# A fused convolution and gated MLP on one core: first chunks' work in larger pieces, a PSUM tile for the warm-up matmuls, and the third chunk's cast ahead of the w_out scaling

## The chip, the cores and the metric

The kernel runs on one core of a Trainium2 chip. The metric is device time in microseconds (us), the median of several runs. For one core no second, slower state of the chip was seen in these runs: all of them are of the state "fast", and only such runs are compared.

Names in the profile: PE is TensorE's matmuls, PEld its weight loads, DVE is VectorE, ACT is ScalarE, POOL is GpSimd, SP is SyncE (which here only issues DMAs). L349 is line 349 of the kernel that was profiled; the changed kernel's lines are shifted by two or more.

## The reference

Two stages. First a causal convolution of seven taps along the sequence, each of eight head groups of 24 channels with its own softmax-normalised weights. Then an MLP with a gate.

```
x: (8, 4096, 192)   weight: (8, 7)   w_in: (192, 2048)   w_out: (2048, 192)   beta: (2048,)
w   = softmax(weight, axis=-1)
out[b, s, c] = sum_k w[c // 24, k] * x_pad[b, s + k, c]      # 6 zero rows in front
h   = out.reshape(32768, 192) @ w_in
g   = h * sigmoid(beta * h)
y   = g @ w_out                                              # (32768, 192), float32
```

## The kernel before

The tokens are worked on in chunks of 512 per half of the batch (two halves at once on the 128 partitions). A step `s` has 16 units `u`. In each unit TensorE computes one block of 128 hidden features of step `s` (`hidden`), and a part of the output of the step before (`output`). The gate is `silu(beta * h)` on ScalarE, so w_out must be divided by beta once; GpSimd does that (`prep_w_out`). The convolution of later chunks is made by VectorE, one instruction a tap, from a transposed bf16 copy of x. That copy is made by DMA: GpSimd issues a cast to a DRAM scratch (`cast`), and SyncE a transposing DMA back (`xpose`).

The first chunk would have to wait long for all of this. So it is split in two half steps (`s = 0` and `s = 1`, 256 tokens each) and its convolution is made by TensorE with diagonal weight matrices; the second chunk's transposes are TensorE's too, and its taps VectorE's. The third chunk (`cast(2)`, `xpose(2)`) is the first to come through the DMA. The code that matters, with cuts marked:

```python
    pc = psum_o.tile([128, 2, TOK], FP32, name="po")

    def fill(n):                                     # warm-up matmuls on zeros
        for _ in range(n):
            nc.tensor.matmul(pc[:, 1, :], zeros[:, 0:128], zeros, start=True, stop=True)

    fill(5)
    ...                                              # six small matmuls: tap weights into pc[:, 0]
    fill(2)
    nc.vector.tensor_copy(ident_b, ident)
    nc.vector.tensor_copy(x0b[:, 0:HB], x0[:, 0:HB])
    cw = consts.tile([128, NG, K], FP32)
    nc.vector.tensor_copy(cw.rearrange("p c k -> p (c k)"), pc[:, 0, 0 : NG * K])
    ...
    for c in range(0, NF, 4):
        prep_w_out(c, 4)                             # GpSimd, w_out / beta
    cast(2)                                          # third chunk
    cast(3)
    ...
    def conv_ops(s):                                 # 21 VectorE instructions, one per tap and group
        ...
    def output(s, u):
        ...
            if fc == NF - 1 and b == 1:              # eviction of a finished output tile
                dst = osb[:, q - 1 : q + 1, :].rearrange("p b d -> p (b d)")
                nc.vector.tensor_copy(dst, po[:, 0, 0 : 2 * D])
                nc.vector.tensor_tensor(dst, po[:, 1, 0 : 2 * D], dst, ALU.add)
        ...
    for s in range(N_ST + 1):
        if s + 2 < N_ST:
            queue.extend(conv_ops(s + 2))
        for u in range(NF):
            if s < N_ST:
                hidden(s, u)
            if s > 0:
                output(s - 1, u)
            next(work, None)                         # first chunks' work in small pieces
            if s > 0:
                pops = 2 - u % 2
            else:
                pops = 0 if u < 5 else 1 if u < 14 else 6
            for _ in range(pops):
                if queue:
                    queue.popleft()()                # puts a tap into VectorE's queue
            if u == 0 and s + 4 < N_CH:
                cast(s + 4)
            if u == 1 and s + 2 < N_CH:
                xpose(s + 2)
```

In these traces VectorE takes up its instructions in the order in which the program gives them: the eviction below, whose data is there at about 35 us, runs at 44.96 us, after the taps that the program puts before it. `pops` decides how many taps of a later chunk stand in VectorE's queue in front of the next eviction.

Of the kernel before, what the change touches and what calls it, by code (L numbers as in the profile page):

```python
# [9 lines left out]
FP32 = mybir.dt.float32  # L10
FP32R = mybir.dt.float32r
BF16 = mybir.dt.bfloat16
# [5 lines left out]
def kernel(  # L18
# [17 lines left out]
    nc = tc.nc  # L36

    B, S, D = x.shape
    H, K = weight.shape
# [3 lines left out]
    NG = D // DG  # L43
    TOK = 512
    NF = F // 128
    PAD = K - 1
    HALO = 16
# [21 lines left out]
    psum_h = ctx.enter_context(  # L69
        tc.tile_pool(name="psum_h", bufs=2, space=bass.MemoryType.PSUM)  # L70
    )
    psum_o = ctx.enter_context(
        tc.tile_pool(name="psum_o", bufs=2, space=bass.MemoryType.PSUM)
    )
# [5 lines left out]
    def new_xt(ch):  # L80
        xt = xt_pool.tile([128, NG, HALO + TOK], BF16, name="xt")
        if ch % CHUNKS == 0:
            nc.vector.memset(xt[:, :, 0:HALO], 0.0)
        xts[ch] = xt
        return xt


    def cast(ch):
        p, c = divmod(ch, CHUNKS)
        r0 = HALO if c == 0 else 0  # L90
        t0 = c * TOK - HALO + r0
        t1 = (c + 1) * TOK
        xd = xd_pool.tile([HALO + TOK, NG, 2, DG], BF16, name="xd")
        for h in range(2):
            nc.gpsimd.dma_start(  # L95
                out=xd[r0:, :, h, :],
                in_=x_v[p, t0:t1, h, :].rearrange("t (c d) -> t c d", c=NG),
            )
        xds[ch] = xd
# [9 lines left out]
    NB = TOK // BLK  # L109
    HB = NB // 2  # L110
    x0 = setup.tile([128, NB, 2, D], FP32)
    x0b = setup.tile([128, NB, 2, D], BF16)
# [16 lines left out]
    zeros = setup.tile([128, TOK], BF16)  # L129
# [17 lines left out]
    def copy_w_in(i):  # L147
        cols = slice(i * FW, (i + 1) * FW)
        nc.vector.tensor_copy(w_in_s[DG : 2 * DG, :, cols], w_in_s[0:DG, :, cols])  # L149
# [12 lines left out]
        fill=0.0,  # L162
# [8 lines left out]
        fill=0.0,  # L171
# [25 lines left out]
    nc.vector.reciprocal(rsum, ssum)  # L197
    nc.vector.tensor_scalar_mul(cw8, cw8, rsum)
    pc = psum_o.tile([128, 2, TOK], FP32, name="po")

    def fill(n):
        for _ in range(n):
            nc.tensor.matmul(pc[:, 1, :], zeros[:, 0:128], zeros, start=True, stop=True)  # L203

    fill(5)
    for c in range(NG):
        nc.tensor.matmul(
            pc[:, 0, c * K : (c + 1) * K],
# [2 lines left out]
            start=True,  # L211
            stop=True,
        )
    fill(2)
    ident_b = setup.tile([128, 128], BF16)
    nc.vector.tensor_copy(ident_b, ident)
    nc.vector.tensor_copy(x0b[:, 0:HB], x0[:, 0:HB])
    cw = consts.tile([128, NG, K], FP32)
    nc.vector.tensor_copy(cw.rearrange("p c k -> p (c k)"), pc[:, 0, 0 : NG * K])

# [3 lines left out]
    def diag_v(c):  # L224
        nc.vector.tensor_tensor(
            diag[:, c, :, :],
            ident.unsqueeze(1).to_broadcast((128, K, 128)),
            cw[:, c, :].unsqueeze(2).to_broadcast((128, K, 128)),
            ALU.mult,
        )  # L230

    def transposes(pt, xb, b0, at, nb):
        for b in range(nb):
            for c in range(NG):
                for h in range(2):
                    nc.tensor.transpose(  # L236
                        pt[h * DG : (h + 1) * DG, c, (at + b) * BLK : (at + b + 1) * BLK],
                        xb[:, b0 + b, h, c * DG : (c + 1) * DG],
                        ident_b,
                    )  # L240

    xt0 = setup.tile([128, NG, HALO + TOK], FP32R)
    nc.vector.memset(xt0[:, :, 0:HALO].bitcast(FP32), 0.0)
    cts = {}

    def diag_tap(s, c, k, pv):
        n = steps[s][2]
        o = HALO - PAD + steps[s][1] + k
        nc.tensor.matmul(  # L249
            pv,  # L250
            diag[:, c, k, :],
            xt0[:, c, o : o + n],
            start=(k == 0),
            stop=(k == K - 1),
        )

    def diag_conv(s, c, pv, ct):
        for k in range(K):
            diag_tap(s, c, k, pv)
        if c == 0:  # L260
            nc.scalar.copy(ct[:, c, 0 : steps[s][2]], pv)  # L261
        else:
            nc.vector.tensor_copy(ct[:, c, 0 : steps[s][2]], pv)

    n0 = HB * BLK
    pt = psum_o.tile([128, NG, n0], BF16, name="po")
    transposes(pt, x0b, 0, 0, HB)
    fill(3)
    diag_v(1)
    nc.scalar.copy(xt0[:, 0:2, HALO : HALO + n0], pt[:, 0:2, :])  # L270
    nc.vector.tensor_copy(xt0[:, 2, HALO : HALO + n0], pt[:, 2, :])
    for k in range(K):
        nc.scalar.mul(diag[:, 0, k, :], ident, cw[:, 0, k : k + 1])
    diag_v(2)
    copy_w_in(0)
    ct = ct_pool.tile([128, NG, TOK], BF16, name="ct")
    cts[0] = ct
    diag_conv(0, 1, psum_h.tile([128, 2, TOK], FP32, name="ph")[:, 0, 0:n0], ct)
    fill(2)
    diag_conv(0, 2, psum_h.tile([128, 2, TOK], FP32, name="ph")[:, 0, 0:n0], ct)  # L280
    beta_p = pc[:, 0, 32 : 32 + NF]
    nc.tensor.transpose(beta_p, beta_q, ident[0:NF, 0:NF])
    beta = consts.tile([128, NF], FP32)
    nc.vector.tensor_copy(beta, beta_p)
    diag_conv(0, 0, psum_o.tile([128, 2, TOK], FP32, name="po")[:, 0, 0:n0], ct)
    beta_r = setup.tile([128, NF], FP32)
    nc.vector.reciprocal(beta_r, beta)
    nc.vector.tensor_copy(x0b[:, HB:NB], x0[:, HB:NB])

    def first_xt():  # L290

        pt = psum_o.tile([128, NG, n0], BF16, name="po")
        transposes(pt, x0b, HB, 0, HB)
        nc.vector.tensor_copy(xt0[:, :, HALO + n0 :], pt)

    def first_conv():

        cts[1] = ct_pool.tile([128, NG, TOK], BF16, name="ct")
        pv = psum_o.tile([128, 4, n0], FP32, name="po")
        for c in range(NG):  # L300
            for k in range(K):
                diag_tap(1, c, k, pv[:, c, :])
                if k % 3 == 2 or k == K - 1:
                    if k == K - 1 and c == NG - 1:
                        nc.vector.tensor_copy(cts[1][:, :, 0:n0], pv[:, 0:NG, :])  # L305
                    yield

    def second_xt():
        xt = new_xt(1)
        pt = psum_o.tile([128, NG, TOK], BF16, name="po")  # L310
        for b in range(NB):
            transposes(pt, x1b, b, b, 1)
            if b == NB - 1:
                nc.vector.tensor_copy(
                    xt[:, :, HALO - PAD : HALO], xt0[:, :, HALO + TOK - PAD :]
                )
                nc.vector.tensor_copy(xt[:, :, HALO:], pt)
            yield
# [3 lines left out]
    def prep_w_out(c0, n):  # L322
        nc.gpsimd.tensor_tensor(  # L323
            w_out_s[:, c0 : c0 + n, :],
            w_out_raw[:, c0 : c0 + n, :],
            beta_r[:, c0 : c0 + n].unsqueeze(2).to_broadcast((128, n, D)),
            ALU.mult,
        )

    for c in range(0, NF, 4):  # L330
        prep_w_out(c, 4)
    cast(2)
    cast(3)


    def conv_ops(s):
        ch, t0, n = steps[s]

        def tap(j, k):
            if j == k == 0:  # L340
                cts[s] = ct_pool.tile([128, NG, TOK], BF16, name="ct")
            o = HALO - PAD + k + t0
            src = xts[ch][:, j, o : o + n]
            dst = cts[s][:, j, 0:n]
            scalar = cw[:, j, k : k + 1]
            if k == 0:
                nc.vector.tensor_scalar_mul(dst, src, scalar)  # L347
            else:
                nc.vector.scalar_tensor_tensor(  # L349
                    out=dst, in0=src, scalar=scalar, in1=dst, op0=ALU.mult, op1=ALU.add  # L350
                )

        return [lambda j=j, k=k: tap(j, k) for k in range(K) for j in range(NG)]
# [59 lines left out]
                )  # L413


    def first_work():

        first_xt()
        copy_w_in(1)
        yield  # L420
        for _ in second_xt():
            yield
        copy_w_in(2)
        for i, _ in enumerate(first_conv()):
            if i == 2:
                copy_w_in(3)
            yield

    work = first_work()
    queue = deque()  # L430
    for s in range(N_ST + 1):
        if s + 2 < N_ST:
# [3 lines that stand above are left out]
                hidden(s, u)  # L436
            if s > 0:
                output(s - 1, u)
            next(work, None)
            if s > 0:  # L440
                pops = 2 - u % 2
            else:
                pops = 0 if u < 5 else 1 if u < 14 else 6
            for _ in range(pops):
                if queue:
                    queue.popleft()()
# [4 lines that stand above are left out]
# [30 lines left out]
```

## Time and profile before

| | before |
|---|---|
| median of the 3 runs | 709.6 us (708.7 to 709.84) |
| profiled span | 708.0 us |
| TensorE busy | 694.0 us (98%) |
| VectorE / ScalarE busy | 78% / 82% |
| first large matmul (step 0) | 13.45 us |
| second half step (step 1) begins | 27.97 us |
| step 2 resumes | 46.16 us |

A kernel whose TensorE is busy 98% can only be gained on where TensorE is idle or slow. The list of waits of TensorE says where; the columns are who waited for whom, us in total, times, and the longest.

```profile
engine line waited for: us in total, times, longest us
PE po L397 <- DVE osb L407: 5.2, 1, 5.2
PE ph L366 <- DVE ct L305: 1.5, 1, 1.5
...
```

The 5.2 us are one wait. The chain of waits (start, us, what) tells what made it. It follows the work back from the end of the program, here from 7.87 to 46.16 us:

```profile
7.87 8.49 DMA w_out_raw<-in_moe_w_out_dram
...
16.50 5.97 POOL w_out_s L323 x4
22.48 1.14 POOL xd L95
23.61 5.14 DMA xd<-in_x_dram
...
28.84 9.91 DMA xt<-xd
...
38.87 0.88 DVE ct L347 x3
39.74 5.30 DVE ct L349 x8
45.04 0.48 DVE osb L406
...
45.55 0.57 DVE osb L407
...
46.16 0.82 PE po L397 x8
```

Read it upwards from the last line. TensorE's output matmuls wait for the eviction L406/L407, which frees their PSUM buffer. The eviction's data had been ready since about 35 us, but in VectorE's queue eleven taps of the third chunk stand in front of it. These wait for the chunk's transpose, that for its cast, and the cast stands in GpSimd's queue behind the scaling of w_out.

VectorE's timeline of the same time (start, us, engine, line, operation, out<-in, count, idle before and releaser) shows both sides of it:

```profile
...
17.34 0.96 DVE L317 COPY xt<-po 128x1536 bf16<-128x1536 bf16 x1 [1.01 <-PE po L236]
18.33 1.61 DVE L149 COPY w_in_s<-w_in_s 64x1536 bf16<-64x1536 bf16 x1
19.97 2.65 DVE L347 TENSOR_SCALAR ct<-xt,cw 128x512 bf16<-128x512 bf16 x2
22.66 0.69 DVE L149 COPY w_in_s<-w_in_s 64x1536 bf16<-64x1536 bf16 x1
...
27.82 8.70 DVE L349 SCALAR_TENSOR_TENSOR ct<-xt,cw,ct 128x512 bf16<-128x512 bf16 x13
38.87 0.88 DVE L347 TENSOR_SCALAR ct<-xt,cw 128x512 bf16<-128x512 bf16 x3 [2.35 <-ACT g L373]
```

It is busy without a gap from 17.34 to 36.5, idle for 2.35 us, and then starts the third chunk's taps. The releaser named there, ScalarE, had been done long before; the DMA transpose landed at 38.74 (in the chain it starts at 28.84 and takes 9.91 us, both rounded), and that is what VectorE waited for. The same copy of w_in takes 1.61 us at 18.33 and 0.69 us at 22.66: in between GpSimd's scaling ended (16.50 to 22.47).

The gap has a second price. TensorE's timeline after it:

```profile
40.16 0.81 PE L366 MATMUL ph<-ct,w_in_s 64*128 64x512 bf16 x6
46.16 0.82 PE L397 MATMUL po<-w_out_s,g 64*128 64x192 bf16 x8 [5.18 <-DVE osb L407]
46.75 1.51 PE L366 MATMUL ph<-ct,w_in_s 64*128 64x512 bf16 x6
...
52.28 0.82 PE L366 MATMUL ph<-ct,w_in_s 64*128 64x512 bf16 x6
```

The same six matmuls take 1.51 us at 46.75 and 0.82 us at 52.28. The granted clock in the windows table is 0.50 from 46.16 to 52.0. The Trainium skill, "TensorE: Matmul & The Clock Gate", section "What's actually happening", says that the array runs at half clock after an idle window of about 3.4 us and at the full one after a busy window; these records agree. Running 5.8 us at half speed costs about 2.9 us, an estimate: half of it.

### The profile page before, as it was taken

How to read it: one execution, taken by the hardware profiler on the slowest of the kernel's cores; microseconds unless marked ns; L12 is line 12 of the kernel's file. 1: busy time of each engine (PE TensorE's matmuls, PEld its weight loads, DVE VectorE, ACT ScalarE, POOL GpSimd, SP SyncE). 2: the span in 40 equal slices, each digit the busy share in tenths (PEclk: the TensorE clock that was granted, in tenths of full speed). 3: DMA queues.
4: the chain of work that ended last, by engine and by line, in shares of the span. 5: the costliest groups of instructions: out<-in, count | busy, mean ns of one | idle time of the engine just before them, and what ended most of it. 6: DMA issues, size and time to landing. Idle time of an engine off the chain costs nothing.

```text
span 708.0 us, 24854 instructions
## 1 busy us (share of the span) xinstructions
PE 694.0 (98%) x11469; PEld 528.7 (75%) x11469; DVE 551.9 (78%) x935; ACT 579.1 (82%) x543; POOL 70.0 (10%) x83
## 2 busy tenths in 40 slices
PE   8979999999999999999999999999999999999997
PEld 5657777777777777777777777777777777777776
DVE  4989988777888777798877788877779887777213
ACT  5759888888888888888888888888888888888881
POOL 6945444000000000000000000000000000000000
PEclk9989999999999999999999999999999999999999
DMA  9999999922213222312222221232221322111012
GB/s 183 107 155 166 172 170 175 134 47 70 60 34 71 69 47 70 68 38 57 69 70 48 69 58 36 69 69 48 69 70 37 57 69 70 47 47 47 24 47 69
DMA packets 181450, 54.57 MB, mean 77 GB/s; under 512 B 146385, under 2 KB 181025, under 8 KB 181345
## 3 DMA queue, kind: packets, MB, share of 16 engines
q0 software_dynamic: 98048, 14.89, 29.4%
q1 hardware_dynamic: 83248, 38.09, 23.1%
q8 instruction: 89, 1.46, 0.9%
q14 instruction: 17, 0.13, 0.1%
q10 hardware_dynamic: 48, 0.01, 0.0%
HBM read 28.98 MB, written 37.29 MB: 94 GB/s over the span
## 4 chain that ended last, share of the span: by engine, by line
PE 93%; DMA 3%; POOL 2%; DVE 1%; issue 0%; POOLq 0%; DVEq 0%; SPq 0%
PE po L397 47%; PE ph L366 46%; DMA xt<-xd 1%; DMA w_out_raw<-in_moe_w_out_dram 1%; POOL w_out_s L323 1%; DVE ct L349 1%; DMA xd<-in_x_dram 1%; POOL w_in_s L142 0%; POOL x1b L117 0%; POOL xd L95 0%; DVE osb L407 0%; DVE osb L406 0%; DVE ct L347 0%; POOL sel L158 0%; POOL sel L167 0%
## 5 line engine op out<-in xcount | busy, mean ns | idle before, releaser
L373 ACT ACTIVATE g<-ph,beta 128x1024 bf16<-128x1024 f32 (+1 forms) x528 | 572.8, 1088 | 106.5 <-PE ph L366 102.2
L397 PEld LDWEIGHTS <-g 64*128 64x128 bf16 x8192 | 370.4, 94 | 108.9 <-issue 7.0
L397 PE MATMUL po<-w_out_s,g 64*128 64x192 bf16 x8192 | 431.5, 243 | 5.2 <-DVE osb L407 5.2
L366 PE MATMUL ph<-ct,w_in_s 64*128 64x512 bf16 (+1 forms) x3168 | 428.9, 372 | 2.0 <-DVE ct L305 1.5
L349 DVE SCALAR_TENSOR_TENSOR ct<-xt,cw,ct 128x512 bf16<-128x512 bf16 x558 | 379.0, 744 | 0.0
L366 PEld LDWEIGHTS <-w_in_s 64*128 64x128 bf16 x3168 | 162.2, 94 | 56.4 <-DVE ct L305 1.8
L406 DVE COPY osb<-po 128x384 f32<-128x384 f32 x128 | 71.4, 558 | 136.3 <-PE po L397 130.5
L407 DVE TENSOR_TENSOR osb<-po,osb 128x384 f32<-128x384 f32 x128 | 71.3, 557 | 4.4
L95 POOL DMA_DIRECT2D xd<-in_x_dram x60 | 54.5, 911 | 45.5 <-DMA xd<-in_x_dram 44.2
L347 DVE TENSOR_SCALAR ct<-xt,cw 128x512 bf16<-128x512 bf16 x93 | 30.2, 379 | 2.4 <-ACT g L373 2.3
L203 PE MATMUL po<-zeros 128*128 128x512 bf16 x12 | 5.9, 629 | 1.3 <-DVE warm L132 1.3
L323 POOL TENSOR_TENSOR w_out_s<-w_out_raw,beta_r 128x768 bf16<-128x768 f32 x4 | 6.0, 1520 | 5.6 <-DMA w_out_raw<-in_moe_w_out_dram 5.6
L249 PE MATMUL po<-xt_145,diag 128*128 128x256 f32 x28 | 6.0, 318 | 0.0
L249 PEld LDWEIGHTS po<-xt_145,diag 128*128 128x128 f32 x28 | 3.9, 188 | 1.9 <-issue 1.9
L149 DVE COPY w_in_s<-w_in_s 64x1536 bf16<-64x1536 bf16 x4 | 3.8, 940 | 0.1
L249 PEld LDWEIGHTS ph<-xt_145,diag 128*128 128x128 f32 x14 | 3.1, 292 | 0.7 <-ACT xt_145 L270 0.3
L249 PE MATMUL ph<-xt_145,diag 128*128 128x256 f32 x14 | 3.6, 419 | 0.0
L203 PEld LDWEIGHTS <-zeros 128*128 128x128 bf16 x12 | 1.2, 130 | 2.6 <-issue 1.3
L261 ACT CAST ct<-po 128x256 bf16<-128x256 f32 x1 | 0.4, 372 | 3.3 <-PE po L249 3.3
L184 POOL DMA_DIRECT2D w_out_raw<-in_moe_w_out_dram x4 | 3.1, 775 | 0.0
L142 POOL DMA_DIRECT2D w_in_s<-in_moe_w_in_dram x4 | 2.6, 673 | 0.8 <-POOLq L465 0.8
L270 ACT CAST xt_145<-po 128x512 fp32r<-128x512 bf16 x1 | 0.6, 585 | 2.3 <-PE po L236 2.3
(45 smaller groups left out, 27.1 us busy)
## 6 DMA issues: line engine op xcount, KB each, us to landing
out_dram<-osb SPq DMA_DIRECT2D x62, 384.0 KB, 3.1
xd<-in_x_dram POOLq DMA_DIRECT2D x54, 198.0 KB, 14.0
w_out_raw<-in_moe_w_out_dram POOLq DMA_DIRECT2D x4, 384.0 KB, 9.1
xd<-in_x_dram POOLq DMA_DIRECT2D x6, 192.0 KB, 15.0
x_83<-in_x_dram SPq DMA_DIRECT2D x4, 192.0 KB, 4.1
w_in_s<-in_moe_w_in_dram POOLq DMA_DIRECT2D x4, 192.0 KB, 7.4
out_dram<-osb SPq DMA_DIRECT2D x4, 192.0 KB, 6.1
xt<-xd SPq DMA_TRANSPOSE x30, 4.9
```

The costliest lines, as they stand in the source:

```text
L95: nc.gpsimd.dma_start(out=xd[r0:, :, h, :], in_=x_v[p, t0:t1, h, :].rearrange("t (c d) -> t c d", c=NG),)
L149: nc.vector.tensor_copy(w_in_s[DG : 2 * DG, :, cols], w_in_s[0:DG, :, cols])
L203: nc.tensor.matmul(pc[:, 1, :], zeros[:, 0:128], zeros, start=True, stop=True)
L249: nc.tensor.matmul(pv, diag[:, c, k, :], xt0[:, c, o : o + n], start=(k == 0), stop=(k == K - 1),)
L323: nc.gpsimd.tensor_tensor(w_out_s[:, c0 : c0 + n, :], w_out_raw[:, c0 : c0 + n, :], beta_r[:, c0 : c0 + n].unsqueeze(2).to_broadcast((128, ...
L347: nc.vector.tensor_scalar_mul(dst, src, scalar)
L349: nc.vector.scalar_tensor_tensor(out=dst, in0=src, scalar=scalar, in1=dst, op0=ALU.mult, op1=ALU.add)
L366: nc.tensor.matmul(ph[:, h, 0:n], w_in_s[rows, j, cols], cts[s][rows, j, 0:n], start=(j == 0), stop=(j == NG - 1),)
L373: nc.scalar.activation(gs[s][:, fc, :, 0:n], ph[:, :, 0:n], AF.Silu, scale=beta[:, fc : fc + 1])
L397: nc.tensor.matmul(po[:, r, b * D : (b + 1) * D], g[rows, fc, h, q * BLK : (q + 1) * BLK], w_out_s[rows, fc, :], start=(fc == 0), stop=(fc ...
L406: nc.vector.tensor_copy(dst, po[:, 0, 0 : 2 * D])
L407: nc.vector.tensor_tensor(dst, po[:, 1, 0 : 2 * D], dst, ALU.add)
```

## The change

Its intent: the first steps are full of small pieces of work between the large matmuls, and each change between them costs TensorE. So the pieces are made larger and fewer. The warm-up matmuls get a PSUM tile of their own, so that the copy of the tap weights need not wait for them. The second half of the first chunk is cast by ScalarE and transposed before the first large matmul. The third chunk's cast is issued ahead of the w_out scaling. The diff, cut to its core:

```diff
     pc = psum_o.tile([128, 2, TOK], FP32, name="po")
+    pf = psum_h.tile([128, 2, TOK], FP32, name="ph")
...
-            nc.tensor.matmul(pc[:, 1, :], zeros[:, 0:128], zeros, start=True, stop=True)
-    fill(5)
+            nc.tensor.matmul(pf[:, 0, :], zeros[:, 0:128], zeros, start=True, stop=True)
+    fill(6)
...
-    fill(2)
     nc.vector.tensor_copy(x0b[:, 0:HB], x0[:, 0:HB])
+    nc.scalar.copy(x0b[:, HB:NB], x0[:, HB:NB])
...
     transposes(pt, x0b, 0, 0, HB)
-    fill(3)
+    fill(2)
...                                   # second half: cast and transposes out of step 0, to here
-    nc.vector.tensor_copy(x0b[:, HB:NB], x0[:, HB:NB])
+    ptb = psum_o.tile([128, NG, n0], BF16, name="po")
+    transposes(ptb, x0b, HB, 0, HB)
+    copy_w_in(0)
-    fill(2)
     diag_conv(0, 2, ...)
     diag_conv(0, 0, ...)
+    nc.vector.tensor_copy(xt0[:, :, HALO + n0 :], ptb)
+    copy_w_in(1)
...
+    cast(2)
     for c in range(0, NF, 4):
         prep_w_out(c, 4)
-    cast(2)
     cast(3)
...                                   # pieces: 12 transposes or 7 taps instead of 6 or 3
+    first_work = {
+        1: more(xt1_work),
+        3: more(xt1_work),
+        4: lambda: copy_w_in(2),
+        5: more(conv1_work),
+        8: lambda: (more(conv1_work)(), copy_w_in(3)),
+        11: more(conv1_work),
+    }
...
-            next(work, None)
+            if s == 0 and u in first_work:
+                first_work[u]()
...
-                pops = 0 if u < 5 else 1 if u < 14 else 6
+                pops = 0 if u < 4 else 1 if u < 12 else 4
```

More of the change, by code (lines that the diff above doesn't have):

```diff
@@ L274 @@
     diag_v(2)
-    copy_w_in(0)
     ct = ct_pool.tile([128, NG, TOK], BF16, name="ct")
@@ L278 @@
     diag_conv(0, 1, psum_h.tile([128, 2, TOK], FP32, name="ph")[:, 0, 0:n0], ct)
-    fill(2)
-    diag_conv(0, 2, psum_h.tile([128, 2, TOK], FP32, name="ph")[:, 0, 0:n0], ct)
     beta_p = pc[:, 0, 32 : 32 + NF]
@@ L284 @@
     nc.vector.tensor_copy(beta, beta_p)
-    diag_conv(0, 0, psum_o.tile([128, 2, TOK], FP32, name="po")[:, 0, 0:n0], ct)
     beta_r = setup.tile([128, NF], FP32)
     nc.vector.reciprocal(beta_r, beta)
-    nc.vector.tensor_copy(x0b[:, HB:NB], x0[:, HB:NB])
-    def first_xt():
-        pt = psum_o.tile([128, NG, n0], BF16, name="po")
-        transposes(pt, x0b, HB, 0, HB)
-        nc.vector.tensor_copy(xt0[:, :, HALO + n0 :], pt)
+    ptb = psum_o.tile([128, NG, n0], BF16, name="po")
+    transposes(ptb, x0b, HB, 0, HB)
+    copy_w_in(0)
+    diag_conv(0, 2, psum_h.tile([128, 2, TOK], FP32, name="ph")[:, 0, 0:n0], ct)
+    diag_conv(0, 0, psum_o.tile([128, 2, TOK], FP32, name="po")[:, 0, 0:n0], ct)
+    nc.vector.tensor_copy(xt0[:, :, HALO + n0 :], ptb)
+    copy_w_in(1)
     def first_conv():
@@ L302, in first_conv @@
                 diag_tap(1, c, k, pv[:, c, :])
-                if k % 3 == 2 or k == K - 1:
-                    if k == K - 1 and c == NG - 1:
-                        nc.vector.tensor_copy(cts[1][:, :, 0:n0], pv[:, 0:NG, :])
-                    yield
+            if c == NG - 1:
+                nc.vector.tensor_copy(cts[1][:, :, 0:n0], pv[:, 0:NG, :])
+            yield
     def second_xt():
@@ L312, in second_xt @@
             transposes(pt, x1b, b, b, 1)
+            if b % 2 == 0:
+                continue
             if b == NB - 1:
@@ L413, in output, with more @@
                 )
-    def first_work():
-        first_xt()
-        copy_w_in(1)
-        yield
-        for _ in second_xt():
-            yield
-        copy_w_in(2)
-        for i, _ in enumerate(first_conv()):
-            if i == 2:
-                copy_w_in(3)
-            yield
-    work = first_work()
+    xt1_work = second_xt()
+    conv1_work = first_conv()
+    def more(work):
+        return lambda: next(work, None)
+    first_work = {
[6 more added lines that the diff above has]
+    }
     queue = deque()
```

## The prediction

> **What bounds the kernel.** TensorE: busy 694.0 of 708.0 us (busy table) and full from 54 us on (stage windows). Only the start can move. The list of waits gives TensorE two long ones after the first large matmul: 1.5 us before 28.0 us (on the second half's convolution) and 5.2 us before 46.16 us. Each is followed by slow matmuls: the eight output matmuls take 0.64 us instead of 0.33, until 31.6 and until 52.1 us (timeline). This fits the Trainium skill, "TensorE: Matmul & The Clock Gate", "What's actually happening": half clock after an idle window, windows of 3.4 us; 31.6 to 52.1 is six of them.
>
> The 5.2 us decide the total. The chain of waits: w_out load lands 16.4, GpSimd scaling 16.5-22.5, cast of the third chunk lands 28.75, its DMA transpose takes 9.9 us to 38.74, then VectorE does 11 convolution taps (38.87-44.96) and the PSUM evictions (to 46.11) queued behind them. VectorE idled 36.5-38.87 for that transpose (the waits view names ScalarE, which was long done). VectorE is busy from 17.34 to 36.5, so other early work hides behind it.
>
> **What the change does.**
> - Cast first: it can be issued at 10.9 instead of 22.4 and should land near 23; even at 9.9 us the transpose ends near 33, before VectorE wants it. The 2.35 us VectorE idle goes.
> - Separate warm-up tile: the weight copy no longer waits for two fills (6.30 -> about 5.4), mostly not realised, because of the next point.
> - x0's second half cast on ScalarE: that load's packets run until nearly 8 us (DMA view), and in ScalarE's order the cast stands before the copy of the first transposes (now 7.09-7.67). I estimate 7.9 + 0.8 (between the 0.58 and 1.09 us that ScalarE takes for 512 and 1024 columns) = 8.7, copy done 9.3: the first diagonal convolution starts near 9.4 instead of 7.88, TensorE idle some 2 us before it. The second half's transposes (0.5-0.85 us, plus about 0.5 waiting for the beta copy to free their PSUM buffer) move ahead of the first large matmul, two fills (0.5) leave. First large matmul: 15-16 us instead of 13.45.
> - Larger pieces: a seven-tap convolution costs 1.0-1.1 us in one piece against 0.55+0.55+0.32 in three; about 1.5 us less TensorE between 13.5 and 26.5. But ScalarE's 16 activations at 0.69 us are 11 us there, so the stage stays near 13 us. VectorE's long stretch starts near 18.5 instead of 17.34.
> - Part of that is absorbed: while GpSimd scales (to 22.5), a VectorE copy took 1.61 us instead of 0.69 and taps 1.1-1.5 instead of 0.35 (Trainium skill, "SBUF — State Buffer", "SBUF: two separate sides": an exclusive port pair). A later start runs fewer of them then.
>
> **Sum.** VectorE ends the second chunk's taps near 37.0 (36.5), goes on at once, evicts near 44.4; TensorE resumes near 44.5 instead of 46.16: -1.7 us. Slow-clock phase after it: shorter or equal, -0.3 on average, +-1. Later nothing changes: 709.6 - 2.0 = 707.6 us, range 705.3 to 709.7. Faster by over 2% 0.01, within 2% 0.98, slower 0.01.
>
> **What would show it.** The transpose issued near 23, landed before 35; no VectorE idle between the second and third chunk's taps; TensorE still idle 4-5 us before about 44.5, ended by the eviction, then slow matmuls; first large matmul later than 13.45 with ScalarE's new cast ending near 8.7.
>
> **What would make it wrong.** The x0 load landing earlier (then the start is 13.0 and the gain nearer 2.5-3 us); the cast's packets delaying the w_out load; the clock staying full over the gap (up to 3 us more gain); w_in's fourth copy coming late and stalling TensorE.

## The result, and the profile after

| | before | after |
|---|---|---|
| median | 709.6 us (708.7 to 709.84, 4 runs) | 707.63 us (707.5 to 708.06, 4 runs) |
| profiled span | 708.0 us | 705.8 us |
| first large matmul | 13.45 us | 15.80 us |
| VectorE's long stretch begins | 17.34 us | 18.66 us |
| third chunk's first tap | 38.87 us | 36.83 us |
| TensorE resumes in step 2 | 46.16 us | 44.12 us |

The ratio is 0.9976 with a 95% interval of 0.9958 to 0.9993. Here and below a ratio is the mean time of one kernel's fast runs over that of the other's of the same rounds, so it is not quite the ratio of the medians that are quoted. The interval does not contain 1, so there is a small gain.

The list of waits and the chain of the kernel after, over the same stretch as above:

```profile
PE po L395 <- DVE osb L405: 4.3, 1, 4.3
PE ph L250 <- ACT xt_146 L271: 2.1, 1, 2.1
PE ph L364 <- ACT g L371: 1.6, 4, 0.5
```

```profile
2.32 5.43 DMA x_83<-in_x_dram
...
8.57 0.59 ACT xt_146 L271
9.20 1.86 PE ph L250 x7
...
15.80 0.52 PE ph L364 x6
...
18.66 0.96 DVE xt L315
...
36.92 0.79 DVE ct L345 x3
...
44.12 0.82 PE po L395 x8
```

The DMAs and the scaling have gone from the end of the chain. In their place stands VectorE's own work, and in front of it the start of the program: TensorE now waits 2.1 us for ScalarE before its first diagonal convolution (L250). ScalarE's timeline shows why:

```profile
7.83 0.83 ACT L218 CAST x0b<-x_83 128x768 bf16<-128x768 f32 x1 [3.08 <-DMA x_83<-in_x_dram]
8.57 0.58 ACT L271 CAST xt_146<-po 128x512 fp32r<-128x512 bf16 x1
```

The new cast L218 waits for the load of x0's second half, and the copy L271 that TensorE needs stands behind it; before, that copy ran at 7.09.

One more thing differs at the start of the two profiles, and no edit aims at it: TensorE's clock. The second and third diagonal convolution of seven matmuls take 1.86 and 1.70 us here (at 11.99 and 13.65), and 1.56 and 1.09 us before (at 10.25 and 11.90). The first clock record in the trace file, at full speed, begins at 15.42 us here and at 11.07 us before; the windows view counts the time ahead of it as full speed.

VectorE's timeline after:

```profile
18.66 0.96 DVE L315 COPY xt<-po 128x1536 bf16<-128x1536 bf16 x1 [2.57 <-PE po L237]
19.65 0.69 DVE L149 COPY w_in_s<-w_in_s 64x1536 bf16<-64x1536 bf16 x1
20.38 2.91 DVE L345 TENSOR_SCALAR ct<-xt,cw 128x512 bf16<-128x512 bf16 x3
...
27.56 9.36 DVE L347 SCALAR_TENSOR_TENSOR ct<-xt,cw,ct 128x512 bf16<-128x512 bf16 x14
36.83 0.88 DVE L345 TENSOR_SCALAR ct<-xt,cw 128x512 bf16<-128x512 bf16 x3
```

There is no idle time before 36.83 any more. The long stretch begins 1.32 us later than before, but ends only 0.4 us later, and the third chunk is tapped 2.04 us earlier, which is just the 2.04 us by which TensorE resumes earlier. After the gap TensorE runs at half clock until 49.55 us (granted clock 0.50 from 44.12 to 49.55), for 5.4 us instead of the 5.9 us of before.

### The profile page after: what moved, and what is told of

The parts are those of the page before. It is cut to its first block, busy times and chain, and to the rows that moved or that the text cites. A ratio compares the mean times of both kernels' runs of the same rounds, so it can differ in the third digit from the quotient of the medians.

```text
span 705.8 us, 24846 instructions
## 1 busy us (share of the span) xinstructions
PE 690.7 (98%) x11465; PEld 530.5 (75%) x11465; DVE 550.1 (78%) x934; ACT 579.2 (82%) x544; POOL 70.3 (10%) x83
## 4 chain that ended last, share of the span: by engine, by line
PE 94%; DVE 4%; DMA 1%; ACT 0%; issue 0%; SPq 0%; ACTq 0%
PE po L395 47%; PE ph L364 46%; DVE ct L347 2%; DMA x_83<-in_x_dram 1%; DVE ct L345 1%; PE ph L250 1%; PE po L250 0%; DVE w_in_s L149 0%; SPq L117 0%; ACT g L371 0%; PE po L237 0%; DVE osb L405 0%; DVE osb L404 0%; DVE xt L315 0%; DVE ct L301 0%
## 5 line engine op out<-in xcount | busy, mean ns | idle before, releaser
L364 PEld LDWEIGHTS <-w_in_s 64*128 64x128 bf16 x3168 | 164.1, 94 | 55.7 <-issue 3.6
L345 DVE TENSOR_SCALAR ct<-xt,cw 128x512 bf16<-128x512 bf16 x93 | 29.9, 377 | 0.0
L250 PE MATMUL ph<-xt_146,diag 128*128 128x256 f32 x14 | 3.7, 439 | 2.1 <-ACT xt_146 L271 2.1
L250 PEld LDWEIGHTS ph<-xt_146,diag 128*128 128x128 f32 x14 | 3.1, 324 | 3.2 <-ACT xt_146 L271 3.0
L204 PE MATMUL ph<-zeros 128*128 128x512 bf16 x8 | 3.8, 627 | 1.3 <-DVE warm L132 1.3
L250 PE MATMUL po<-xt_146,diag 128*128 128x256 f32 x28 | 5.0, 326 | 0.0
L250 PEld LDWEIGHTS po<-xt_146,diag 128*128 128x128 f32 x28 | 4.3, 224 | 0.6 <-issue 0.6
L218 ACT CAST x0b<-x_83 128x768 bf16<-128x768 f32 x1 | 0.8, 831 | 3.1 <-DMA x_83<-in_x_dram 3.1
```

What stands on the lines that cost most here:

```text
L204: nc.tensor.matmul(pf[:, 0, :], zeros[:, 0:128], zeros, start=True, stop=True)
L250: nc.tensor.matmul(pv, diag[:, c, k, :], xt0[:, c, o : o + n], start=(k == 0), stop=(k == K - 1),)
L345: nc.vector.tensor_scalar_mul(dst, src, scalar)
L364: nc.tensor.matmul(ph[:, h, 0:n], w_in_s[rows, j, cols], cts[s][rows, j, 0:n], start=(j == 0), stop=(j == NG - 1),)
```

## The experiments

The theory: the gain is the 2.35 us for which VectorE waited for the third chunk (theory A), and everything else in the first 40 us hides behind VectorE, whose order of work decides when TensorE may go on. The rival: the gain comes from the faster start and the larger pieces (B). Each experiment was timed in five rounds against the kernel before on the same chip. Those that came in one call are in one group; times of different groups are compared by their ratios to before.

### The parts of the change, one at a time

**cast_only** is the kernel before with one edit:

```diff
+    cast(2)
     for c in range(0, NF, 4):
         prep_w_out(c, 4)
-    cast(2)
     cast(3)
```

> Before plus only the third chunk's cast ahead of the w_out scaling. Theory A (the gain is the 2.35 us that VectorE sat idle for the transposed third chunk): no VectorE idle at 36.5 us, eviction near 43.7, TensorE resumes near 43.8 instead of 46.16, total about 707.2 us (706.4 to 708.0), so the whole of the gain or a little more. Rival B (the gain is the faster start and the larger pieces): about 709.6, within 0.5.

Measured: 706.61 us (706.17 to 707.65), ratio 0.9959 [0.9947, 0.9971]. VectorE reaches the third chunk at 36.83 without a gap, TensorE resumes at 44.09. The one moved line gives all of the gain, and B falls as its cause. (A wait of VectorE would stand in brackets at the end of this line.)

```profile
36.83 0.86 DVE L347 TENSOR_SCALAR ct<-xt,cw 128x512 bf16<-128x512 bf16 x3
```

**cast_late** is the other way round: the changed kernel with the cast put back behind the scaling.

> The changed kernel with the cast put back behind the scaling. Theory A: the transposed chunk lands near 39, VectorE idles about 2 us before its first tap on it, TensorE resumes near 46.3, total about 709.6 us (708.9 to 710.3). Rival B: the gain stays, about 707.6.

Measured: 711.25 us (709.38 to 713.45), ratio 1.0023 [1.0007, 1.0038]: slower than before. The gain goes with the cast, as A says, but the loss is larger than was expected:

```profile
42.19 0.88 DVE L345 TENSOR_SCALAR ct<-xt,cw 128x512 bf16<-128x512 bf16 x3 [4.60 <-DMA xt<-xd]
```

VectorE waits 4.6 us, and this time the profile names the DMA. The scaling began later in this run (17.58 instead of 16.91 us after, when the w_out load landed), the transpose was issued at 30.44 and took 11.6 us to land, against 9.9 in the kernel before and 6.9 in the kernel after. In these profiles the transposes that were issued later took longer; that later casts already queued are the reason is plausible and was not tested. The estimate of 39 us for its landing had taken the 9.9 us over.

**own_fill_tile** is the kernel before with the PSUM tile `pf` alone.

> Before with only the warm-up matmuls in a PSUM tile of their own. The weight copy runs at about 6.3 us only if it waits for the fills because of the tile; here it runs near 5.4. TensorE's own queue still runs the fills between, so the first large matmul stays near 13.45 (13.0 to 13.5) and the total at 709.6 us within 0.5, because the transposed chunk lands no earlier. Rival B: 0.9 us less.

Measured: 709.65 us (708.84 to 710.61), ratio 0.9993 [0.9979, 1.0007]. The copy of the weights runs at 5.35 instead of 6.30 us, as intended, and the first large matmul is at 13.59: VectorE then waits 1.06 us for ScalarE instead. A real wait was removed, and nothing was behind it.

**x0_later** is the changed kernel with ScalarE's cast moved behind the copy that TensorE waits for:

```diff
-    nc.scalar.copy(x0b[:, HB:NB], x0[:, HB:NB])
...
     nc.scalar.copy(xt0[:, 0:2, HALO : HALO + n0], pt[:, 0:2, :])
+    nc.scalar.copy(x0b[:, HB:NB], x0[:, HB:NB])
```

> The changed kernel with ScalarE's cast of x0's second half moved behind its copy of the first transposes. First diagonal convolution near 7.0 us instead of 9.20, first large matmul near 13.4 instead of 15.80. Theory A with the port pair: VectorE's long stretch starts 2 us earlier but three or four more of its operations then meet GpSimd's scaling (16.9 to 22.9), so the taps end only 0.3 to 0.6 us earlier and the total is about 707.2 us. Rival C (the later start costs its full 2 us): about 705.4.

Measured: 706.4 us (705.16 to 706.66), ratio 0.9949 [0.9937, 0.996]. The first large matmul is at 11.70 us, 4.1 us earlier than in the changed kernel, and VectorE's long stretch begins at 15.27 instead of 18.66, 3.4 us earlier. But the third chunk's taps begin only 1.0 us earlier, at 35.82, and TensorE resumes at 43.09. More came through than the 0.3 to 0.6 us of the expectation, much less than the full start. Not all of the 4.1 us is the moved cast. The first diagonal convolution of the changed kernel, and then of this one:

```profile
9.20 1.86 PE L250 MATMUL ph<-xt_146,diag 128*128 128x256 f32 x7 [2.08 <-ACT xt_146 L271]
```

```profile
6.37 1.08 PE L249 MATMUL ph<-xt,diag 128*128 128x256 f32 x7 [0.24 <-DVE diag L225]
```

It begins 2.8 us earlier, and the three convolutions take 1.08, 1.11 and 1.04 us instead of 1.86, 1.86 and 1.70: 2.2 us less, because TensorE is at full clock from 4.13 us on (first clock record). Against this stands a wait of 1.19 us at 8.80 for the moved cast. Up to 4.13 us TensorE has the same instructions at the same times in both kernels, so the edit can hardly have brought the early full clock; that it helped to keep it is possible and not shown (evict_first, below, has ScalarE's cast in the old place, reached full clock at 4.74 us and lost it at 8.15, in a wait of 3.17 us for ScalarE). In which of the unprofiled runs the clock was full so early is not known.

Where the other 2.4 us of VectorE's earlier start went can be read off its timeline:

```profile
16.97 2.11 DVE L345 TENSOR_SCALAR ct<-xt,cw 128x512 bf16<-128x512 bf16 x3
19.00 1.95 DVE L347 SCALAR_TENSOR_TENSOR ct<-xt,cw,ct 128x512 bf16<-128x512 bf16 x1
20.98 1.84 DVE L149 COPY w_in_s<-w_in_s 64x1536 bf16<-64x1536 bf16 x1
```

Alone, the three take 0.88, 0.74 and 0.69 us. Here, during GpSimd's scaling (17.46 to 23.88), they take 2.11, 1.95 and 1.84, and one more tap at 22.86 takes 1.58: 4.4 us more than alone. In the changed kernel only the three L345 taps are slowed, by 2.0 us. The difference is the missing 2.4 us.

**no_scaling** takes the suspected cause away: GpSimd's scaling is left out of the changed kernel and w_out is cast to bf16 on its way in. Its output is wrong, which doesn't matter for the time.

> The changed kernel without GpSimd's scaling (w_out is cast on its way in; the result is wrong on purpose). Port pair theory: the three first taps take 0.9 us together instead of 2.91, the eviction comes 2 us earlier, TensorE resumes near 42.1, total about 705.5 us. Rival (those taps are slow for another reason): taps 2.9 us and about 707.6.

Measured: 705.17 us (704.76 to 705.97), ratio 0.993 [0.9917, 0.9943].

```profile
18.71 0.69 DVE L149 COPY w_in_s<-w_in_s 64x1536 bf16<-64x1536 bf16 x1
19.43 1.25 DVE L333 TENSOR_SCALAR ct<-xt,cw 128x512 bf16<-128x512 bf16 x3
```

The three taps take 1.25 us instead of 2.91, and TensorE resumes at 42.49. So most of their slowness was the scaling. The total does not measure it alone: in this profile TensorE's gap before 42.49 was 2.50 us, and the six matmuls after it took 0.83 us, so the half-speed phase is missing too. The rest, 1.25 against 0.88, is not explained by it; GpSimd issues DMAs at that time in this kernel.

### The order of VectorE's work

If taps that stand in front of the eviction are what makes TensorE wait, then moving them behind it should remove the gap itself, where the change only shortened it. **evict_first** is the changed kernel with:

```diff
-            if s > 0:
+            if s == 1:
+                pops = 0 if u < 7 else 1
+            elif s == 2:
+                pops = 1
+            elif s > 0:
                 pops = 2 - u % 2
```

> The changed kernel, but the third chunk's taps are not put into VectorE's queue before the first output eviction of the second stage, and fewer of them before the next two. Theory A: the eviction runs right after the second chunk's taps (36.8), TensorE goes on at 39 without the gap of 4.3 us, its clock stays full (another 2.5 us), total about 700.3 us (699 to 702). Rival D (VectorE's total work early is the bound, not its order): the stall moves to a later stage, total 706 to 708.

Measured: 700.44 us (700.21 to 701.12), ratio 0.9872 [0.9857, 0.9886]. VectorE evicts right after the second chunk's taps, and TensorE goes through without a gap and at full speed:

```profile
37.03 0.55 DVE L404 COPY osb<-po 128x384 f32<-128x384 f32 x1
37.61 0.56 DVE L405 TENSOR_TENSOR osb<-po,osb 128x384 f32<-128x384 f32 x1
38.09 0.87 DVE L345 TENSOR_SCALAR ct<-xt,cw 128x512 bf16<-128x512 bf16 x3
```

```profile
38.92 0.83 PE L364 MATMUL ph<-ct,w_in_s 64*128 64x512 bf16 x6
39.57 0.51 PE L395 MATMUL po<-w_out_s,g 64*128 64x192 bf16 x8
39.90 0.83 PE L364 MATMUL ph<-ct,w_in_s 64*128 64x512 bf16 x6
```

No wait for an eviction is left in TensorE's list. The rival of this experiment (VectorE has too much work, whatever its order) falls: the taps were moved, none was removed.

**before_evict_first** is the kernel before with the same edit, the cast left behind the scaling.

> The kernel before with only the queue order of evict_first. Theory A: without the eviction behind them the taps may wait for the transposed chunk at no cost: TensorE goes on near 40.9 without a long gap, total about 702 us (700.5 to 703), so the cast's place no longer matters. Rival: the chunk still lands at 38.7 and the next stage waits for its taps, total above 706.

Measured: 701.85 us (701.76 to 701.96), ratio 0.9882 [0.9868, 0.9897]. The eviction ends at 37.6. VectorE still waits for the third chunk (2.75 us, until 40.38), but nothing that TensorE needs stands behind that wait, and TensorE's list has no long wait in step 2:

```profile
37.07 0.56 DVE L407 TENSOR_TENSOR osb<-po,osb 128x384 f32<-128x384 f32 x1
40.38 1.24 DVE L347 TENSOR_SCALAR ct<-xt,cw 128x512 bf16<-128x512 bf16 x3 [2.75 <-DMA xt<-xd]
```

So the wait for the transpose was costly only through the queue.

**cast_evict_first** adds the cast's move to that. It is thus evict_first_x0_later, below, without the larger pieces, the fill tile and ScalarE's cast.

> Before plus the cast ahead of the scaling plus the queue order of evict_first; so evict_first_x0_later without the larger pieces, the fill tile and x0's cast on ScalarE. If VectorE's order hid what these parts gain, they show now: TensorE reaches the first half-filled stage's end near 40 us instead of 36.6, total 701 to 702 us against 698.3. If they are worth nothing in themselves: about 698.5.

Measured: 700.67 us (699.94 to 703.96), ratio 0.9858 [0.9841, 0.9874], with a wide scatter; in the profiled run, the slowest, TensorE was at half speed from 28.95 until about 35 us. It is nearer to the first branch of the expectation (701 to 702) than to the second (698.5). It overlaps with before_evict_first (0.9868 to 0.9897), so whether the cast's place is worth anything once the order is right stays open.

**evict_first_x0_later** puts both edits on the changed kernel.

> evict_first and x0_later together. If evict_first takes away the VectorE bound, TensorE's start shows: the second stage begins when VectorE has copied its convolution, 0.3 to 1 us earlier, total 0.5 to 2 us below evict_first, about 699 us. If the port pair eats the earlier start here too, the same as evict_first within 0.5.

Measured: 698.28 us (697.81 to 699.11), ratio 0.9834 [0.9819, 0.985]. That is 2.2 us below evict_first and 2.4 us below cast_evict_first by the medians, 2.7 and 1.7 us by the ratios (0.0038 and 0.0024 of 710). Together, the larger pieces, the fill tile and the earlier start are worth about this much once VectorE's order no longer hides them: step 0 now starts at 11.76 instead of 13.48 and step 2 begins at 36.63. Which of these parts is worth it stays open, since neither the larger pieces nor the moved cast was run alone; and TensorE's clock was full from 4.25 us in this profile and from 11.09 in that of cast_evict_first, a share that is not separated.

**copy_before_taps** adds one more change of order, of three taps that stood in front of the copy of the second half's convolution:

```diff
-                pops = 0 if u < 4 else 1 if u < 12 else 4
+                pops = 0 if u < 4 or 8 <= u < 12 else 1 if u < 8 else 5
```

> evict_first_x0_later, with no taps put into VectorE's queue between the first and the last piece of the second half's convolution, so that its copy runs about 2.9 us earlier. The second stage starts near 24.4 instead of 26.06, where ScalarE's activations end. But VectorE's work up to the eviction (35.2 to 36.3) is the same, so TensorE waits for the eviction instead: total about 698 us, within 0.7 of evict_first_x0_later. If the copy's place were the bound: 696.7.

Measured: 697.18 us (696.43 to 699.4), ratio 0.9818 [0.9798, 0.9838], the fastest of all by its median, though its interval overlaps with that of evict_first_x0_later. The expectation was wrong in one step: it held VectorE's work up to the eviction to be the same. The eviction ended 0.9 us earlier. Evict_first_x0_later first, then copy_before_taps, at the same time of the scaling (which ends at 23.3 and 23.2 us):

```profile
22.24 1.58 DVE L347 SCALAR_TENSOR_TENSOR ct<-xt,cw,ct 128x512 bf16<-128x512 bf16 x1
```

```profile
22.16 0.96 DVE L301 CAST ct<-po 128x768 bf16<-128x768 f32 x1
23.04 0.74 DVE L347 SCALAR_TENSOR_TENSOR ct<-xt,cw,ct 128x512 bf16<-128x512 bf16 x1
```

The copy comes out of PSUM and takes its usual 0.95 us beside the scaling; the tap, run after it, takes 0.74 instead of 1.58.

### The whole change against its best part

**after_again** and **cast_only_again** repeat the changed kernel and cast_only in the same rounds.

> The changed kernel once more, in the same rounds as cast_only_again, to separate the two: 707.6 us (707.2 to 708.2) again. In the profiles of both VectorE reaches the third chunk's first tap at 36.83 us and TensorE resumes at 44.1; what differs is the half-speed phase after it, which ends near 49.1 here and near 47.3 there.

> 706.6 us again (706.1 to 707.7), so about 1 us less than the changed kernel: the parts other than the cast then cost a little as they stand. If the two come out within 0.4 us of each other, the difference was of the chip or the batch.

Measured: 707.28 us (706.54 to 708.36), ratio 0.9971 [0.9955, 0.9986], against 706.38 us (706.08 to 707.43), ratio 0.9957 [0.9942, 0.9972]. The means differ by 0.8 us, in the same direction as in the first group, but the intervals overlap: the other parts as they stand gain nothing, and perhaps cost a little. In both profiles TensorE resumes within 0.1 us of the same time (44.09 and 44.20). What differs is the clock after the gap. In cast_only_again TensorE reached the gap later (41.3 against 39.1 us, after a half-speed phase from 28.9 to 32.4), was idle only 2.9 us and came back at full speed; in after_again it was idle 5.0 us and the next 3.6 us were almost all slow. That a later arrival can be the faster one for this reason is seen in these two profiles, not shown for the medians. The mean clock that each run of after_again lists points to the slow phases too, but not cleanly: two runs at 0.996 took 706.54 and 706.66 us and three at 0.994 took 707.74 to 708.36, yet one at 0.989 took 706.83. (The ends of the slow phases in the expectation, 49.1 and 47.3, are 49.55 and 47.18 in the clock records.)

## Why the prediction was right

The time was predicted as 707.6 us and measured as 707.63. That the two agree to 0.03 us is luck: the four runs spread over 0.56 us, and the median of the kernel before moves between 709.59 and 710.7 us from group to group. What holds is the mechanism. Point by point:

- **TensorE's early gap decides, through VectorE's queue.** Right: evict_first removes the gap by order alone and wins 7 us more.
- **The cast can be issued at 10.9 and the third chunk is no longer waited for.** Right. The cast's second half was held up on GpSimd until 13.82 (1.9 us of waiting for the landing of w_in's load), which had not been foreseen; the chunk still landed in time for a transpose issued at 23.56. The transpose took 6.9 us where 9.9 had been allowed for.
- **The fill tile's 0.9 us is mostly not realised.** Right; own_fill_tile shows it worth nothing by itself as well.
- **ScalarE's cast delays the start.** Right, and nearly to the number: the cast ended at 8.66 (8.7 predicted), the first diagonal convolution began at 9.20 (9.4), TensorE idled 2.08 us (2), the first large matmul came at 15.80 (15 to 16). That the first large matmul fell into the range is in part luck. The sum had allowed 0.5 us for a wait for the beta copy, and TensorE shows none; it had no term for the clock, and the second and third convolution took 0.9 us longer than in the profile before. x0_later shows the price in the total: about 1.9 us by the ratios (0.9976 and 0.9949, of different groups, with intervals that just overlap), and the clock of the start is in it.
- **Step 0 stays near 13 us.** Right: 12.7 us, from 15.80 to 28.47, with ScalarE the engine waited for.
- **A later start meets less of the scaling.** Right in its size, not shown in its reason. The w_in copy took 0.69 instead of 1.61 us, and the long stretch, 1.3 us later at its start, ended 0.4 us later. But this copy (19.65 to 20.34) lies inside the scaling, which itself ran 0.4 us later (16.91 to 22.88). With the same code up to there it took 1.12 us in after_again and 1.79 in evict_first; the copy and the three taps together took 3.60 us here, 4.04 and 3.86 there. So how much is absorbed changes from run to run.
- **Sum.** TensorE resumed at 44.12 where 44.5 was predicted, so the gain there was 2.04 us instead of 1.7. The slow phase after it was 0.4 us shorter (5.43 instead of 5.87), which is worth about 0.2 us (0.3 predicted). Together 2.3 us, against 2.2 us of difference between the two spans and 2.0 us between the medians.

What the prediction missed is not in its sum but in its view: it priced the parts of the change and did not ask which part should be left out, or whether the gap could be removed instead of shortened. One line of the change gives the whole gain (cast_only, 3.0 us by the medians of its group), and another edit, of the order, gives almost three times that on the same kernel (before_evict_first, 8.3 us).

## What to carry to other kernels

When an engine waits for another one's result, look at what stands in front of that result in the other engine's queue, before making anything in that queue faster: in the kernel before, moving the eviction ahead of eleven taps won 8 us where feeding these taps earlier won 3. When work is handed to an engine that has time, look at what it must wait for and at what stands behind it in that engine's order; a cast of 0.83 us, with the load that it waited for, held the start up by 2 us. And where the next instruction is held up by another engine's work, try to put one there that is not: in copy_before_taps this brought the eviction 0.9 us forward in the profile, though its gain in the total is within the noise.

## What the Trainium skill lacked or had wrong

- "SBUF — State Buffer", section "Who interferes with whom", says that a VectorE instruction with two SBUF inputs contends with a GpSimd instruction that reads SBUF, and that one with at most one SBUF input outside the two-port modes does not. The runs agree: taps with two inputs took 1.58 and 1.95 us during the scaling instead of 0.74, and a copy out of PSUM kept its 0.95 us. The section gives no size for such taps, and the use that can be made of the second case, a PSUM copy put where a tap would be held up, follows from it but is not spelled out (copy_before_taps: eviction 0.9 us earlier).
- "TensorE: Matmul & The Clock Gate", section "HAM oscillation — how this bites in real kernels", puts its rule as no idle gaps of over about 3.4 us. Shorter ones were followed by half speed here: in the kernel before, a gap of 1.49 us at 26.5 was followed by output matmuls at 0.64 us instead of 0.33 until 31.6, while gaps of 1.85 us (cast_only, at 26.5) and 2.90 us (cast_only_again, at 41.3) were not. What share of a window must be busy is not stated, and these runs don't settle it.
- The same page, section "What's actually happening", gives about 3.4 us of sustained work for warming up. Here the first matmul is at 1.26 us and TensorE is busy 11.4 of the 12.2 us up to 13.45; yet in the kernel before the seven matmuls of a diagonal convolution still took 1.56 us at 10.25 and 1.09 us only at 11.90. With the same code up to there, before_evict_first had the second one at 1.18 us and its first large matmul at 12.11 instead of 13.45 us. The granted clock in the windows view reads 1.00 through all of it, because the first clock record begins only at 11.07 us (8.12 in before_evict_first, 15.42 in the kernel after): this start is seen in the matmuls' durations, not in that column.
- No page that was looked up says how long a DMA transpose of one such chunk takes beside casts on the same engines: 5.1 us (cast_only), 6.9 (after), 9.9 (before) and 11.6 (cast_late) for the same transfer.
